# Sums by accumulating DMAs replaced by additions on GpSimd, in a gated scan with a feed-forward layer

## The chip, the cores and the metric

The kernel runs on one core of a Trainium2 chip. Five engines run their own instruction queues in order: TensorE (PE, with its weight loads PEld), VectorE (DVE), ScalarE (ACT), GpSimd (POOL) and SyncE (SP). An instruction that waits holds up all that stand behind it on its engine. The metric is the device time of one execution in microseconds (us).

## The reference

The first half is a gated scan along 6080 time steps, for 2 sequences of 256 channels; the second half is a feed-forward layer of 2048 hidden units on the 12160 resulting rows.

```python
sig = 1 / (1 + exp(-f_logit))
f = lower_bound + (1 - lower_bound) * sig
for t in range(S):
    h = f[:, t] * h + (1 - f[:, t]) * x[:, t]
    y[:, t] = h
h = y.reshape(B * S, D) @ w_in
g = h * clip(h + 3, 0, 6) / 6
out = g @ w_out
```

## The kernel before

Rows are handled as runs of 512 time steps (480 at the end) of one sequence; two runs of the same steps of both sequences make a pair. The first four runs go through the layer one by one (`direct`). Each of the ten later pairs goes through a 2x2 block product in seven multiplications where a plain one needs eight (`seven`), for the first product, and, for three of the eight blocks of hidden units in all pairs but the first, for the second product too (`chain`, `seven_in_banks`). Such a scheme multiplies sums and differences of blocks: t1, t2, t3 and t4, each made of blocks of x (the scan's result, tiles `xt`) or of g (the gated hidden units, tiles `r`).

Each operand is split into two parts of lower precision (`split`, `split_flat`): ACT writes the high part (`xhi`, `ghi`, `bhi`), DVE the rest (`xlo`, `glo`, `blo`), and PE multiplies three combinations. A product leaves PE in a bank of its accumulation memory (`bank`); ACT and DVE add or copy banks for the scheme (lines 628 to 640) and apply the gate (`gate`, lines 503 and 505), which frees the bank for a later product.

The sums are made in place, in one of two ways:

- t1 and t2 of g are additions by DVE (`ON_DVE`, line 811).
- t3 and t4 of g and all four sums of x are accumulating DMAs, issued by POOL (`add_into`, line 262). There are 4 per pair for x, 128 columns by 512 (480) values, 40 in all; and 4 per chain for g, two of them twice as long (1024 or 960 values), 36 in all.

The order of instructions on every engine is written by a planner (`ordered`): every job has an engine, a planning cost and a due time, and the planner walks through time, each engine taking the ready job that is due first. PE's jobs come in the order of the program's loops, with times to match. For an accumulating DMA the planner allows an issue (`ISSUE_ADD`), its bytes on a shared bus, a landing time and `LATE`, and it keeps the descriptors in flight below a limit. At the start PE runs multiplications of zeros (line 924) while it has nothing to do; their number follows from the plan.

Of the kernel before, what the change touches and what calls it, by code (L numbers as in the profile page):

```python
# [16 lines left out]
ALU = mybir.AluOpType  # L17
P = 128
BANK = 512
# [73 lines left out]
def dve_cost(n, per=1.0):  # L93
    return (151 + per * n) / 0.96


def pe_cost(n, count):
    return count * (n + 32) / 2.4

# [5 lines left out]
    return count * (4 * n + 64) / 2.4  # L105


HOP = {"PE": 230, "ACT": 70, "DVE": 70, "SP": 0, "POOL": 0}
ISSUE = 480
ISSUE_ADD = 1000  # L110
LATE = 1000
ON_DVE = {("t1", 0), ("t1", 1), ("t2", 0), ("t2", 1)}
AHEAD = 8000
DIRECT = 4
# [2 lines left out]
SCRATCH = 512  # L117
LANDING = 1700
SLOW_START = 6500
BYTES_PER_NS = 390  # L120
# [3 lines left out]
def ordered(jobs):  # L124


    for j in jobs:
        for b in j.bufs:
            if b.before is not None:
                j.needs.extend(u for u in b.before.users if u is not j)  # L130
    for j in jobs:
        j.needs = list(dict.fromkeys(j.needs))
        j.after = []
    for j in jobs:
        for n in j.needs:
            n.after.append(j)
    left = {j: len(j.after) for j in jobs}
    stack = [j for j in jobs if not left[j]]
    while stack:
        j = stack.pop()  # L140
        late = min((d.due for d in j.after), default=1e9) - HOP[j.engine] - j.cost
        if j.moves:
            late -= LANDING + j.moves / BYTES_PER_NS + (LATE if j.engine == "POOL" else 0)
        if j.at is None:
            j.due = late
        for n in j.needs:
            left[n] -= 1
            if not left[n]:
                stack.append(n)

    def early(j):
        return max(0.0, j.due - j.ahead) if j.due < 5e8 else 0.0
    missing = {j: len(j.needs) for j in jobs}
    ready = {e: [] for e in HOP}
    free = dict.fromkeys(ready, BEGIN)
    bus = 0.0
    flying = []
    number = {j: i for i, j in enumerate(jobs)}
    for j in jobs:
        if not missing[j]:  # L160
            ready[j.engine].append((early(j), j))
    order = []
    while any(ready.values()):
        best = None
        for e, waiting in ready.items():
            if waiting:
                start = max(free[e], min(r for r, _ in waiting))
                if best is None or start < best[0]:
                    best = (start, e)
        start, e = best  # L170
        could = [x for x in ready[e] if x[0] <= start]
        pick = min(could, key=lambda x: (x[1].due, number[x[1]]))
        ready[e].remove(pick)
        j = pick[1]
        if e == "POOL":
            room = SCRATCH // 16 - 1
            pieces = 1 + P // 16 * -(-j.moves // (2 * P * 2048))
            while flying and sum(k for _, k in flying) + pieces > room:
                start = max(start, flying.pop(0)[0])
        j.start = start  # L180
        free[e] = end = start + j.cost
        if j.moves:
            bus = max(bus, end)
            slow = min(j.moves / 250, max(0, SLOW_START - bus))
            bus += slow + (j.moves - 250 * slow) / BYTES_PER_NS
            end = bus + LANDING
            if e == "POOL":
                end += LATE
                flying.append((end, pieces))
        j.end = end  # L190
        order.append(j)
        for d in j.after:
            missing[d] -= 1
            if not missing[d]:
                at = max(n.end + (HOP[n.engine] if n.engine != d.engine else 0) for n in d.needs)
                ready[d.engine].append((max(at, early(d)), d))
    assert len(order) == len(jobs)
    return order
# [18 lines left out]
def gated_scan_then_ffn(  # L217
# [8 lines left out]
    nc = tc.nc  # L226
# [24 lines left out]
    def job(*args, **kw):  # L251
        j = Job(*args, **kw)
        jobs.append(j)
        return j
# [2 lines left out]
        engine = nc.scalar if queue == "ACT" else nc.sync  # L257
        return job(queue, ISSUE, lambda: engine.dma_start(out(), src), bufs=[buf] if buf else [], moves=size, ahead=EARLY)

    def add_into(size, out, src, needs, bufs, ahead=None):  # L260

        return job("POOL", ISSUE_ADD, lambda: nc.gpsimd.dma_start(out=out(), in_=src(), accum_op=ALU.add),  # L262
                   needs, bufs, moves=2 * size, ahead=ahead)

    r_ft = Ring(work, "ft", FT, [P, KD, BANK], F32)
    r_xt = Ring(work, "xt", 2, [P, KD, BANK], F32)
# [152 lines left out]
    def split(src, hi, lo, cut, n, needs, flip=False, to=None):  # L419

        to = to or cut

        def high():
            if flip:
                nc.scalar.mul(to(hi), cut(src), -1.0)  # L425
            else:
                nc.scalar.copy(to(hi), cut(src))  # L427

        def low():
            if flip:  # L430
                nc.vector.scalar_tensor_tensor(out=to(lo), in0=cut(src), scalar=-1.0, in1=to(hi).bitcast(F32),  # L431
                                               op0=ALU.mult, op1=ALU.subtract)
            else:
                nc.vector.tensor_tensor(to(lo), cut(src), to(hi).bitcast(F32), op=ALU.subtract)  # L434
        c = job("ACT", act_cost(n), high, needs, [src, hi])
        return [c, job("DVE", dve_cost(n), low, [c], [src, hi, lo])]
# [16 lines left out]
    def prep_pair(h, h2):  # L453


        n = runs[h][2]
        assert runs[h][0] == 0 and runs[h2][0] == 1
        _, xt, one = scan_x(h, [(0, n)])
        _, xt2, two = scan_x(h2, [(0, n)])
        ss, ss2 = one[0][-1], two[0][-1]  # L460

        def cut(k):
            return lambda b: b.get()[:, k, :n]

        def sum_into(buf, k, buf2, k2, needs):
            return [add_into(4 * n * P, lambda: cut(k)(buf), lambda: cut(k2)(buf2), needs, {buf, buf2})]
        both = lambda b: b.get()[:, :, :n]
        whole = lambda b: b.get()[:, :n]
        own, t12, t34 = [(r_xhi.new(), r_xlo.new()) for _ in range(3)]
        end = r_bhi.new(), r_blo.new()  # L470
        d_own = split(xt, *own, both, KD * n, ss)
        j1 = sum_into(xt, 0, xt2, 0, [*ss, *ss2, *d_own])
        d1 = split(xt, *t12, cut(0), n, j1)
        j3 = sum_into(xt2, 0, xt2, 1, [*ss2, *j1])
        j2 = sum_into(xt, 0, xt2, 1, [*d1, *ss2])
        d2 = split(xt, *t12, cut(0), n, j2, to=cut(1))
        d3 = split(xt2, *t34, both, KD * n, j3)
        j4 = sum_into(xt, 1, xt, 0, [*j2, *d_own])
        d4 = split(xt, *end, cut(1), n, j4, flip=True, to=whole)
        for name, bufs, at, done in (("b11", own, cut(0), d_own), ("b21", own, cut(1), d_own), ("b22", t34, cut(1), d3),  # L480
                                     ("t1", t12, cut(0), d1), ("t2", t12, cut(1), d2),
                                     ("t3", t34, cut(0), d3), ("t4", end, whole, d4)):
            operands[h, name] = bufs, at
            o_done[h, name] = done
# [5 lines left out]
    def pe(n, count, emit, needs, bufs, cost=pe_cost):  # L490
        j = job("PE", cost(n, count), emit, needs, bufs, at=clock[0])
        clock[0] += cost(n, count)
        return j
# [308 lines left out]
    def chain(h, h2):  # L802

        n = runs[h][2]
        r_ghi.left = r_glo.left = None
        made = g_done[h]
        flat = lambda b: b.get()[:, :(b.shape[1] // BANK) * n]

        def sum_into(name, z, out, x, needs, ahead=None):
            if (name, z) in ON_DVE:  # L810
                return job("DVE", dve_cost(n * (out.shape[1] // BANK)), lambda: nc.vector.tensor_tensor(flat(out), flat(out), flat(x), op=ALU.add),
                           needs, [out, x])
            return add_into(4 * (out.shape[1] // BANK) * n * P, lambda: flat(out), lambda: flat(x), needs, [out, x], ahead)
        ops = {}

        def operand(name, w, z, needs, flip):
# [5 lines left out]
        every = range(len(PARTS))  # L822
        d11 = [operand("b11", w11, z, g11, True) for z in every]
        t1 = [[sum_into("t1", z, w11[z], w12[z], [*g12[z], *d11[z]])] for z in every]
        dt1 = [operand("t1", w11, z, t1, False) for z in every]
        t3 = [[sum_into("t3", z, w12[z], w22[z], [*g22[z], *t1[z]], AHEAD)] for z in every]
# [78 lines left out]
    for _ in range(5):  # L905
        order = ordered(jobs)
        end = max(j.end for j in order)
        if best is None or end < best[0]:
            best = end, order, [(j.start, j.end) for j in order]
        for j in jobs:  # L910
            if j.at is not None:
                j.at = j.due = j.start
# [44 lines left out]
```

## Time and profile before

| | us |
|---|---|
| median of 3 runs (988.11 to 988.68) | 988.17 |
| the profiled execution | 988.75 |
| its span, from the first to the last instruction | 987.0 |
| PE busy | 980.0 |
| DVE busy | 842.2 |
| ACT busy | 705.3 |
| POOL busy | 66.9 |

The span is what the profile's views divide up; the profiled execution's own time has 1.75 us beside it. An engine's busy time is not a bound by itself: what matters is which engine the others end up waiting for. PE's clock is granted at full speed throughout the page's forty slices.

### The profile page before, as it was taken

The page shows a single profiled execution, that of the slowest core. Times are in us where ns is not written, and L with a number is a line of the kernel's source. Part 1 is how long each engine was busy: PE and PEld are TensorE (multiplying, and loading weights), DVE is VectorE, ACT ScalarE, POOL GpSimd, SP SyncE. Part 2 cuts the span into 40 slices and gives each one's busy share as a digit, 9 for nine tenths or more (in the row PEclk, how much of TensorE's full clock was granted, in tenths as well). Part 3 has the DMA queues.
Part 4 walks back from the last instruction along what each step waited for, and adds up shares of the span by engine and source line. Part 5 has one row for each costly group of instructions (what it writes and reads, how often), then busy time and mean ns, then how long its engine had stood idle before and what let it go on. Part 6 is the DMA issues. An engine that isn't in the chain of part 4 may idle for free.

```text
span 987.0 us, 11965 instructions
## 1 busy us (share of the span) xinstructions
PE 980.0 (99%) x4316; PEld 806.4 (82%) x4316; DVE 842.2 (85%) x1150; ACT 705.3 (71%) x1150; POOL 66.9 (7%) x80
## 2 busy tenths in 40 slices
PE   8999999999999999999999999999999999999998
PEld 3788888888888888888888888888888888888887
DVE  7999998679778979988988998898898898898883
ACT  7975666577667767768668767777776866876762
POOL 0000001000000100011011011010010101101100
PEclk9999999999999999999999999999999999999999
DMA  8842032021141233124116125224222412502301
GB/s 340 287 146 80 23 105 65 2 86 35 30 138 34 59 100 76 43 68 125 33 32 161 33 43 139 40 57 122 50 54 54 125 31 45 148 23 48 81 11 41
DMA packets 36843, 79.21 MB, mean 80 GB/s; under 512 B 3504, under 2 KB 9648, under 8 KB 36784
## 3 DMA queue, kind: packets, MB, share of 16 engines
q1 hardware_dynamic: 25424, 53.87, 16.1%
q0 software_dynamic: 10944, 24.32, 13.2%
q8 instruction: 34, 0.56, 0.2%
q10 hardware_dynamic: 416, 0.26, 0.1%
q14 instruction: 25, 0.20, 0.1%
HBM read 41.67 MB, written 12.45 MB: 55 GB/s over the span
## 4 chain that ended last, share of the span: by engine, by line
PE 98%; DVE 1%; ACT 0%; issue 0%
PE bank L649 51%; PE bank L538 38%; PE bank L604 8%; PE bank L614 1%; PE bank L535 0%; DVE xt L396 0%; DVE xt L406 0%; ACT r L384 0%; ACT r L393 0%; DVE r L505 0%; DVE r L577 0%; ACT last L413 0%
## 5 line engine op out<-in xcount | busy, mean ns | idle before, releaser
L503 ACT ACTIVATE r<-bank 128x512 f32<-128x512 f32 (+1 forms) x304 | 178.7, 591 | 118.6 <-PE bank L649 85.2
L505 DVE SCALAR_TENSOR_TENSOR r<-r,bank 128x512 f32<-128x512 f32 (+1 forms) x304 | 203.9, 676 | 48.1 <-ACT r L503 46.4
L649 PE MATMUL bank<-xhi,wst 128*128 128x512 f32 (+1 forms) x640 | 233.0, 387 | 0.0
L538 PE MATMUL bank<-ghi,whi 128*128 128x512 f32 (+1 forms) x548 | 212.7, 388 | 0.0
L538 PE MATMUL bank<-glo,whi 128*128 128x512 f32 (+1 forms) x548 | 212.5, 388 | 0.0
L538 PE MATMUL bank<-ghi,wlo 128*128 128x512 f32 (+1 forms) x548 | 212.4, 388 | 0.0
L431 DVE SCALAR_TENSOR_TENSOR glo<-r,ghi 128x1024 fp32r<-128x1024 f32 (+3 forms) x125 | 131.3, 1052 | 16.3 <-ACT ghi L425 16.1
L649 PEld LDWEIGHTS bank<-xhi,wst 128*128 128x128 f32 x640 | 120.1, 188 | 23.8
L427 ACT CAST ghi<-r 128x1024 fp32r<-128x1024 f32 (+3 forms) x107 | 98.7, 931 | 45.7 <-PE bank L649 31.1
L649 PE MATMUL bank<-xlo,wst 128*128 128x512 f32 (+1 forms) x320 | 123.8, 387 | 0.0
L425 ACT ACTIVATE ghi<-r 128x1024 fp32r<-128x1024 f32 (+3 forms) x125 | 115.3, 924 | 10.6 <-PE bank L538 5.3
L434 DVE TENSOR_TENSOR glo<-r,ghi 128x1024 fp32r<-128x1024 f32 (+3 forms) x107 | 113.8, 1073 | 10.5 <-ACT ghi L427 10.3
L538 PEld LDWEIGHTS bank<-ghi,wlo 128*128 128x128 f32 x548 | 102.8, 188 | 20.8 <-DVE wlo L311 0.2
L538 PEld LDWEIGHTS bank<-glo,whi 128*128 128x128 f32 x548 | 102.8, 188 | 20.7
L538 PEld LDWEIGHTS bank<-ghi,whi 128*128 128x128 f32 x548 | 102.9, 188 | 20.6 <-issue 0.2
L640 DVE TENSOR_TENSOR bank<-bank,e 128x512 f32<-128x512 f32 (+1 forms) x80 | 55.2, 690 | 21.0 <-PE bank L649 14.7
L262 POOL DMA_DIRECT2D xt<-xt x40 | 35.2, 880 | 556.4 <-ACT last L413 357.2
L649 PEld LDWEIGHTS bank<-xlo,wst 128*128 128x128 f32 x320 | 60.1, 188 | 12.0
L649 PE MATMUL bank<-ghi,wlo 128*128 128x512 f32 (+1 forms) x180 | 69.6, 387 | 0.0
L649 PE MATMUL bank<-ghi,whi 128*128 128x512 f32 (+1 forms) x180 | 69.6, 387 | 0.0
L649 PE MATMUL bank<-glo,whi 128*128 128x512 f32 (+1 forms) x180 | 69.6, 387 | 0.0
L638 DVE SCALAR_TENSOR_TENSOR e<-bank,e 128x512 f32<-128x512 f32 (+1 forms) x80 | 54.3, 679 | 10.4 <-PE bank L649 9.6
(105 smaller groups left out, 1494.2 us busy)
## 6 DMA issues: line engine op xcount, KB each, us to landing
outT<-r SPq DMA_DIRECT2D x40, 256.0 KB, 2.2
xt<-xT SPq DMA_DIRECT2D x18, 512.0 KB, 5.3
ft<-fT SPq DMA_DIRECT2D x17, 512.0 KB, 3.8
xt<-xt POOLq DMA_DIRECT2D x32, 256.0 KB, 3.2
wst<-w SPq DMA_DIRECT2D x14, 512.0 KB, 4.0
r<-r POOLq DMA_DIRECT2D x14, 512.0 KB, 4.8
wst<-w SPq DMA_DIRECT2D x14, 511.5 KB, 4.9
r<-r POOLq DMA_DIRECT2D x14, 256.0 KB, 3.4
```

The lines of the kernel that those rows point to most:

```text
L262: return job("POOL", ISSUE_ADD, lambda: nc.gpsimd.dma_start(out=out(), in_=src(), accum_op=ALU.add), needs, bufs, moves=2 * size, ahead=ahead)
L425: nc.scalar.mul(to(hi), cut(src), -1.0)
L427: nc.scalar.copy(to(hi), cut(src))
L431: nc.vector.scalar_tensor_tensor(out=to(lo), in0=cut(src), scalar=-1.0, in1=to(hi).bitcast(F32), op0=ALU.mult, op1=ALU.subtract)
L434: nc.vector.tensor_tensor(to(lo), cut(src), to(hi).bitcast(F32), op=ALU.subtract)
L503: b = job("ACT", act_cost(n, psum=True), lambda: nc.scalar.activation(piece(r, i, n), src.get()[:, :n], AF.Relu, bias=3.0, scale=-1.0 if n ...
L505: return job("DVE", dve_cost(n), lambda: nc.vector.scalar_tensor_tensor(out=piece(r, i, n), in0=piece(r, i, n), scalar=6.0, in1=src.get()[ ...
L538: nc.tensor.matmul(bank.get()[:, :n], wt[f][:, D + m * P:D + (m + 1) * P], piece(g, half, n), start=(start and i == 0), stop=(stop and i = ...
L604: nc.tensor.matmul(ph.get()[:, o:e], wt[f][:, k * P:(k + 1) * P], x[h].get()[:, k, o:e], start=(i == 0), stop=(i == len(ops) - 1),)
L638: nc.vector.scalar_tensor_tensor(out=o, in0=x, scalar=-1.0, in1=y, op0=ALU.mult, op1=ALU.subtract)
L640: nc.vector.tensor_tensor(o, x, y, op=ALU.add)
L649: nc.tensor.matmul(bank.get()[:, :n], wt(), x(), start=(start and z == 0 and i == 0), stop=(z == len(parts) - 1 and i == 2), skip_group_ch ...
```

## The change

The 76 accumulating DMAs become additions (`tensor_tensor`) that POOL carries out itself, with two operands from the on-chip buffer and the result in place of the first. In the planner their bytes, landing time, `LATE` and the limit on descriptors go; a POOL job now has a cost of its own (`pool_cost`) and a handover time.

```diff
+def pool_cost(n):
+    return 300 + 2.6 * n / 1.2
...
-HOP = {"PE": 230, "ACT": 70, "DVE": 70, "SP": 0, "POOL": 0}
+HOP = {"PE": 230, "ACT": 70, "DVE": 70, "SP": 0, "POOL": 70}
...
-ISSUE_ADD = 1000
-LATE = 1000
...
-    def add_into(size, out, src, needs, bufs, ahead=None):
-
-        return job("POOL", ISSUE_ADD, lambda: nc.gpsimd.dma_start(out=out(), in_=src(), accum_op=ALU.add),
-                   needs, bufs, moves=2 * size, ahead=ahead)
+    def add_into(n, out, src, needs, bufs, ahead=None):
+
+        return job("POOL", pool_cost(n), lambda: nc.gpsimd.tensor_tensor(out(), out(), src(), op=ALU.add),
+                   needs, bufs, ahead=ahead)
...
-            return [add_into(4 * n * P, lambda: cut(k)(buf), lambda: cut(k2)(buf2), needs, {buf, buf2})]
+            return [add_into(n, lambda: cut(k)(buf), lambda: cut(k2)(buf2), needs, {buf, buf2})]
...
-            return add_into(4 * (out.shape[1] // BANK) * n * P, lambda: flat(out), lambda: flat(x), needs, [out, x], ahead)
+            return add_into((out.shape[1] // BANK) * n, lambda: flat(out), lambda: flat(x), needs, [out, x], ahead)
```

The planner's numbers decide the order on every engine, so rows move on the others too. Three places follow; the number behind a name is that of the buffer.

POOL, the four sums of one chain (tiles `r`) and the first two sums of the next pair (tiles `xt`), before:

```order
L262 DMA r_3651<-r_3682 128x1024
L262 DMA r_3746<-r_3767 128x512
L262 DMA r_3799<-r_3736 128x512
L262 DMA r_3689<-r_3583 128x1024
L262 DMA xt_3787<-xt_3860 128x512
L262 DMA xt_3860<-xt_3860 128x512
```

and after:

```order
L255 TENSOR_TENSOR r_3617<-r_3617,r_3641 128x1024
L255 TENSOR_TENSOR r_3748<-r_3748,r_3765 128x512
L255 TENSOR_TENSOR r_3653<-r_3653,r_3599 128x1024
L255 TENSOR_TENSOR r_3793<-r_3793,r_3726 128x512
L255 TENSOR_TENSOR xt_3807<-xt_3807,xt_3882 128x512
L255 TENSOR_TENSOR xt_3882<-xt_3882 128x512
```

The sums keep their places but for the last two of the chain, which change order.

ACT at the same chain, where it splits t3 (`ghi_3939` of `r_3651`) and t4 (`ghi_3957` of `r_3689`, `ghi_3967` of `r_3799`), before:

```order
L393 ACTIVATE ft_3763<-ft_3763,gb,ga 128x512
L425 ACTIVATE ghi_3939<-r_3651 128x1024
L503 ACTIVATE r_3952<-bank_0_3873 128x512
L503 ACTIVATE r_3926<-e_3895 128x512
L427 CAST ghi_3957<-r_3689 128x1024
L427 CAST ghi_3967<-r_3799 128x512
L628 ACTIVATE bank_0_3975<-bank_0_3959 128x512
```

and after, with t3 in `ghi_3933` and t4 in `ghi_3952` and `ghi_3961`:

```order
L418 ACTIVATE ghi_3933<-r_3617 128x1024
L496 ACTIVATE r_3939<-bank_0_3872 128x512
L420 CAST ghi_3952<-r_3653 128x1024
L386 ACTIVATE ft_3791<-ft_3791,gb,ga 128x512
L420 CAST ghi_3961<-r_3793 128x512
L621 ACTIVATE bank_0_3969<-bank_0_3957 128x512
```

One gate (L503 of `r_3926`) and the scan's line 393 have moved from ahead of the split of t4 to other places; the split stands nearer to its sum.

ACT at the start of the program, where it prepares the weights (`xhi_110`, `xhi_117`; lines 300, 302) and the gate of the second run (`r_121`; lines 384, 393), before:

```order
L310 CAST whi_69<-xhi_110 128x256 [waits DVE_49]
L300 ACTIVATE xhi_117<-xhi_117 128x256 [waits DMAHW7_49,DMAHW0_49]
L302 ACTIVATE xhi_117<-xhi_117 128x256 [waits Activation_49]
L413 ACTIVATE last<-xt_108 128x1 [waits DVE_49]
L384 ACTIVATE r_121<-r_121 128x1024 [waits DMAHW1_49]
L393 ACTIVATE r_121<-r_121,gb,ga 128x512 [waits Activation_49]
```

and after:

```order
L303 CAST whi_69<-xhi_110 128x256 [waits DVE_49]
L377 ACTIVATE r_117<-r_117 128x1024 [waits DMAHW7_49]
L386 ACTIVATE r_117<-r_117,gb,ga 128x512 [waits Activation_49]
L293 ACTIVATE xhi_119<-xhi_119 128x256 [waits DMAHW1_49,DMAHW0_49]
L295 ACTIVATE xhi_119<-xhi_119 128x256 [waits Activation_49]
```

The second run's gate goes ahead of the second block of weights; SP issues their loads in the same new order, and two of the 41 multiplications of zeros on PE are gone.

## Rows read from the trace of the kernel before

**Rows 1.** The page: busy time, share of the span, instructions.

```profile
PE 980.0 (99%) x4316; PEld 806.4 (82%) x4316; DVE 842.2 (85%) x1150; ACT 705.3 (71%) x1150; POOL 66.9 (7%) x80
```

**Rows 2.** Waits of PE: for whom, us in total, times, longest.

```profile
PE bank L614 <- DVE xhi L307: 1.6, 1, 1.6
PE bank L924 <- DVE spare_w L918: 1.2, 1, 1.2
PE bank L614 <- DVE r L505: 0.5, 1, 0.5
```

**Rows 3.** Busy time by stretch, one pair: PE, PEld, DVE, ACT, POOL, clock.

```profile
449.00:528.00 79.00, 79.00 (x350) 65.46 (x349) 69.72 (x89) 58.38 (x94) 7.00 (x8) 1.00 0.30 72
```

**Rows 4.** POOL's groups: busy us, mean ns, idle before them and its releaser.

```profile
L262 POOL DMA_DIRECT2D xt<-xt x40 | 35.2, 880 | 556.4 <-ACT last L413 357.2 <-ACT r L503 101.3 <-DVE xlo L434 42.1
L262 POOL DMA_DIRECT2D r<-r x36 | 31.5, 875 | 313.5 <-DVE r L505 198.8 <-DVE glo L434 88.3 <-DVE glo L431 26.4
```

**Rows 5.** DMA issues by POOL: count, KB each, median us to landing.

```profile
xt<-xt POOLq DMA_DIRECT2D x32, 256.0 KB, 3.2
r<-r POOLq DMA_DIRECT2D x14, 512.0 KB, 4.8
```

**Rows 6.** ACT's longest waits for DMAs.

```profile
ACT ghi L427 <- DMA r<-r: 0.4, 1, 0.4
```

**Rows 7.** DVE's groups by form: busy us, mean ns.

```profile
L505 DVE SCALAR_TENSOR_TENSOR r<-r,bank 128x512 f32<-128x512 f32 x256 | 173.1, 682 | 38.7 <-ACT r L503 37.3
L505 DVE SCALAR_TENSOR_TENSOR r<-r,e 128x512 f32<-128x512 f32 x64 | 43.6, 683 | 3.9 <-ACT r L503 3.1
L811 DVE TENSOR_TENSOR r<-r,r 128x1024 f32<-128x1024 f32 x14 | 17.1, 1222 | 0.3
L811 DVE TENSOR_TENSOR r<-r,r 128x512 f32<-128x512 f32 x14 | 9.7, 691 | 0.4
```

**Rows 8.** Timeline of POOL from 419 to 461: start, us, instruction.

```profile
419.65 0.89 POOL L262 DMA_DIRECT2D xt<-xt  x1 [3.98 <-DVE xlo L434]
...
440.77 0.88 POOL L262 DMA_DIRECT2D r<-r  x1 [16.63 <-DVE r L505]
...
460.69 0.87 POOL L262 DMA_DIRECT2D r<-r  x1 [2.79 <-DVE glo L431]
```

**Rows 9.** Timeline of DVE around the three.

```profile
419.16 0.68 DVE L505 SCALAR_TENSOR_TENSOR r<-r,e 128x512 f32<-128x512 f32 x1
419.76 1.22 DVE L434 TENSOR_TENSOR glo<-r,ghi 128x1024 fp32r<-128x1024 f32 x1
420.90 0.68 DVE L505 SCALAR_TENSOR_TENSOR r<-r,bank 128x512 f32<-128x512 f32 x1
...
441.24 1.32 DVE L505 SCALAR_TENSOR_TENSOR r<-r,bank 128x512 f32<-128x512 f32 x2
...
460.28 0.70 DVE L640 TENSOR_TENSOR bank<-bank,e 128x512 f32<-128x512 f32 x1 [0.51 <-PE bank L649]
460.89 0.68 DVE L431 SCALAR_TENSOR_TENSOR glo<-r,ghi 128x512 fp32r<-128x512 f32 x1
...
464.36 0.69 DVE L638 SCALAR_TENSOR_TENSOR e<-bank,e 128x512 f32<-128x512 f32 x1 [0.40 <-PE bank L649]
...
466.10 0.68 DVE L505 SCALAR_TENSOR_TENSOR r<-r,bank 128x512 f32<-128x512 f32 x1
```

**Rows 10.** Timeline of PE: the products that take those banks next.

```profile
423.36 0.39 PE L649 MATMUL bank<-xhi,whi 128*128 128x512 f32 x1
...
467.56 0.39 PE L649 MATMUL bank<-xhi,wst 128*128 128x512 f32 x1
```

**Rows 11.** Timeline of ACT at the start.

```profile
10.33 0.45 ACT L300 ACTIVATE xhi<-xhi 128x256 f32<-128x256 f32 x1
...
11.91 1.04 ACT L384 ACTIVATE r<-r 128x1024 f32<-128x1024 f32 x1
```

**Rows 12.** Timeline of PE: the second run's first product.

```profile
18.06 1.99 PE L614 MATMUL bank<-xt,xhi 128*128 128x512 f32 x4 [0.46 <-DVE r L505]
```

More of the change, by code (lines that the diff above doesn't have):

```diff
@@ L142, in ordered @@
         if j.moves:
-            late -= LANDING + j.moves / BYTES_PER_NS + (LATE if j.engine == "POOL" else 0)
+            late -= LANDING + j.moves / BYTES_PER_NS
         if j.at is None:
@@ L156, in ordered @@
     bus = 0.0
-    flying = []
     number = {j: i for i, j in enumerate(jobs)}
@@ L174, in ordered @@
         j = pick[1]
[L175 to L179, printed above, removed]
         j.start = start
@@ L186, in ordered @@
             end = bus + LANDING
-            if e == "POOL":
-                end += LATE
-                flying.append((end, pieces))
         j.end = end
```

## Prediction

> **What bounds the kernel now.** I read the page first: PE is busy for 980.0 of 987.0 us, DVE for 842, ACT for 705, POOL for 67 [rows 1]. Busy PE alone proves little, so the waits of PE came next: it waits three times in all, 3.3 us together, and always on line 614 or 924, which stand in the first 20 us [rows 2]. From then on PE is never without an operand or a bank. The view by stretches says the same of one pair in the middle: in 79.0 us PE is busy for 79.0 at a granted clock of 1.00, and DVE for 69.7, so DVE has 9.3 us to spare per pair [rows 3]. Two things follow. What is taken off POOL and the DMA queues can return almost nothing, since PE waits for neither. And whatever makes DVE or ACT later than PE can bear is paid in full, since PE has no slack to make it up.
>
> **What the change removes.** 76 issues on POOL go, 40 for x and 36 for g, some 0.88 us each, 66.7 us together [rows 4], and the transfers that landed 3.2 us (short) or 4.8 us (long) after issue [rows 5]. POOL sat idle for most of the span and nobody waited for its issues; of the landings ACT waited for one, for 0.4 us [rows 6], and PE for none. I count the removal at nothing: the cover is PE's own work, and were it gone it would show up among PE's waits.
>
> **What it adds on POOL.** 76 additions: 40 for x and 18 for g of 512 (480) values, 18 for g of 1024 (960). No row shows POOL adding. The nearest row from below is DVE's addition of the same shape, 0.69 and 1.22 us [rows 7]; from above, the DMA's landing, 3.2 and 4.8 us, since the plan lived with it. These lie far apart and I take the middle on a scale of ratios, 1.5 us (the root of 0.69 times 3.2) and 2.4 us (the root of 1.22 times 4.8). POOL would be busy for 58 x 1.5 + 18 x 2.4 = 130 us, 13% of the span, so it is far from a bound, and a sum would be ready earlier than a DMA's. In the order ACT's splits stand closer behind their sums than before, so some of that lead is spent, but I see no term in it: the sum costs half of what it did.
>
> The Trainium skill, GPSIMD Engine Reference, section 3 (Performance versus the Vector engine), gives 4497 ns for a two-input addition of 2048 values and a slope of about 2.6 cycles per value; scaled down that is an estimate of 1.2 and 2.3 us, and by it the sum below would be 6.2 us in place of 7.1. No run here shows it yet.
>
> **What it adds on DVE.** This is the term. POOL reads two operands from the on-chip buffer for 1.5 to 2.4 us at a time, right beside DVE instructions that do the same. Whether both can run at once the trace does not show, as POOL computes nothing in it. The lower end is nothing: they run side by side, as ACT and DVE do now. The upper end is that a DVE instruction with both operands in the buffer stands until the addition is over; one with an operand in a bank (r<-r,bank; 682 ns, against 683 ns for r<-r,e today [rows 7]) would go on. I take the upper end, as the one that PE would notice, and keep the lower as a rival.
>
> The Trainium skill, SBUF — State Buffer, section "Who interferes with whom", states this upper end: VectorE's second operand comes through a read interface shared with GpSimd, and the one that comes second waits for the whole instruction of the other. No row here can confirm it.
>
> Laid over the trace, a long sum that starts at 460.69 [rows 8] would end at 463.09. DVE's line 640 at 460.28 has an operand in a bank and goes on; the next, glo<-r,ghi at 460.89, has not, and stands for 463.09 - 460.89 = 2.20 us, with everything behind it. DVE's idle 0.40 us before 464.36 takes that to 1.80. Line 505 at 466.10 ends at 466.78 and frees a bank that PE's product at 467.56 takes [rows 9, 10]: a lead of 0.78. So PE stands for 1.80 - 0.78 = 1.02 us there.
>
> A short sum at 419.65 [rows 8] would start when r<-r,e has finished, at 419.84, and end at 421.34; glo<-r,ghi at 419.76 would stand for some 1.5 us. Line 505 at 420.90 would end 1.5 us after 421.58, and PE takes its bank at 423.36: a lead of 1.78, and PE waits for nothing [rows 9, 10]. I count short sums at nothing; the cover is this lead, and without it each costs up to 1.5 us.
>
> There are nine chains, with two long sums each; one of the two meets splits and short leads as at 460.69, the other, here at 440.77, falls on gates with an operand in a bank, 441.24 and on, and holds up nothing [rows 8, 9]. Seven chains are of 512 columns; the last two, of 480, have shorter sums, and I take them at nothing. The sum is 7 x 1.02 = 7.1 us.
>
> **What moves at the start.** ACT takes the second run's gate (11.91) ahead of the second block of weights (10.33), up to 1.6 us earlier [rows 11], and PE's wait of 0.46 us before 18.06 hangs on that run [rows 12]. Against it the second block of weights comes later, 1.04 us and more, and its products with it. Between a gain of 1.6 + 0.46 = 2.1 us and a loss of about 1.0 I take nothing.
>
> So the profiled execution's 988.75 (987.0 of span and 1.75 beside it) would become 995.9; it lay 0.6 above the median of 988.17, and from the median the forecast is 988.17 + 7.1 = 995.3.
>
> **The rivals.**
>
> *Side by side, or covered.* POOL's additions do not hold DVE up, or its leads of up to 1.8 us cover all of it. For it: the one short place above is covered, and DVE has 9.3 us to spare per pair against 6 x 1.5 + 2 x 2.4 = 13.8 us of POOL's work, only part of which meets DVE instructions of the wrong kind. Against it: the place at 460.69, which comes in every chain. Time: 988.2.
>
> *DVE runs full.* If nearly all of the 13.8 us per pair is DVE's to stand, it exceeds the 9.3 us to spare by 4.5, and nine pairs cost 9 x 4.5 = 40 us: about 1028. The point from which it decides is a stall of 9.3 us per pair, an average of 1.2 us for each of the eight sums. Against it: DVE spends a good part of its time on instructions with an operand in a bank, 173.1 us on r<-r,bank of 512 values alone [rows 7], and my short place and long place give 1.5 and 2.2 only because they meet the other kind at once.
>
> *Faster.* The start alone: the second run's gate comes 1.6 us earlier, PE's 0.46 us go, and every later product moves up by 2.1 us, while the sums cost nothing: 986.1. It decides only if the new load order keeps the weights in time. For it: two multiplications of zeros fewer. Against it: PE's longest wait at the start, 1.6 us, is for weights (line 307) [rows 2], which this order delays.
>
> **How the numbers follow.** Forecast 0.57, side by side or covered 0.27, DVE full 0.10, faster 0.06. The low end is the rival of the start less some of its gain, 986.8. The high end lets one short sum in each of ten pairs find no lead: 988.17 + 7.1 + 10 x 1.5 = 1010. About 1.5 in 10 is left out, most of it above. What this kernel's measurement can tell from no change is about 0.2%, 2 us. The second case and a small part of the first stay within that, 0.30; the rival of the start goes beyond it by very little, 0.05 faster; the rest is slower, 0.65.
>
> **What would show each step.** Right: 76 POOL additions of 1 to 3 us; among DVE's groups those with two operands in the buffer (glo<-r,ghi at lines 424 and 427, r<-r,e) have a higher mean or a tail of single long ones beside POOL's rows, while r<-r,bank keeps 0.68 us; PE has waits for DVE at line 642 in the chains, about 1 us each, after 195 us. Wrong by the first rival: the DVE means stand and PE's waits remain those of the first 20 us. Wrong by the second: DVE busy near 79 us per pair, and PE waits at most sums. What else would make it wrong: additions of over 3 us on POOL, so that ACT's splits wait for POOL with the gates queued behind them, or a first addition that comes late for a reason no row here shows.

## The result, and the profile after

The changed kernel takes 994.64 us (median of four runs, 994.55 to 994.69); the kernel before, run beside it, takes 988.25 (988.11 to 988.68). The ratio is 1.0064 with a 95% interval of 1.0046 to 1.0081: 6.4 us slower, well beyond the 0.2% that can be told here. The profiled run of the changed kernel took 994.67, of which 992.8 are its span. The code has become seven lines shorter above all that matters here, so line 642 below is line 649 of before, 498 is 505, 424 and 427 are 431 and 434, 631 and 633 are 638 and 640, and the additions stand on line 255.

The page's first line answers to [rows 1]:

```profile
PE 985.8 (99%) x4314; PEld 804.5 (81%) x4314; DVE 883.0 (89%) x1150; ACT 707.1 (71%) x1150; POOL 144.9 (15%) x80
```

DVE has gained 40.8 us with not one instruction more, POOL 78. PE is "busy" for 5.8 us more with two records fewer. That is a trap: a product's record lasts 0.39 us while the next starts 0.23 us behind it, so a start that comes up to 0.16 us late leaves no gap between the records and counts as busy, and so does part of any longer delay. The waits of PE hardly show the loss; those of its weight loads, which wait for the same banks, do. First PE, which answers to [rows 2], then PEld; each row is for whom it waited, us in total, times, longest:

```profile
PE bank L917 <- DVE spare_w L911: 1.2, 1, 1.2
PE bank L642 <- DVE r L498: 0.7, 1, 0.7
```

```profile
PEld bank L642 <- DVE r L498: 3.9, 10, 1.2
PEld bank L642 <- DVE e L631: 2.7, 7, 0.4
```

The kernel before has no wait of PE or PEld on this line for DVE behind the start. Now there are two kinds above all: ten for line 498 and seven for line 631, both of which read a bank that a product wants next.

The chain of work that ended last gives the sizes. Its largest pieces start once in each pair of runs, at the same product. In the kernel before it is:

```profile
289.53 27.20 PE bank L649 x120
...
448.68 27.20 PE bank L649 x120
...
766.92 27.20 PE bank L649 x120
```

and in the changed kernel:

```profile
289.21 26.65 PE bank L642 x117
...
449.96 18.36 PE bank L642 x81
468.34 8.50 PE bank L642 x36
...
772.40 26.95 PE bank L642 x117
```

From the first to the last of these, six pairs take 477.39 us before and 483.19 after, 5.80 more: 0.97 us a pair on the mean, and nearly all of the loss. Where the piece of 120 is broken in two, at 468.34, something has stepped in between.

Where the loss arises can be read product by product. The order on PE has moved with the plan too: at 1209 of the 4275 places behind the multiplications of zeros, another product stands than before. But run 2 below, which takes the time of before (988.30), has the changed kernel's order at all 4275, so each product's start in the changed kernel can be set against its start there. The changed kernel falls behind in two kinds of place:

| where | falls behind there (us) | together (us) |
|---|---|---|
| the sums of x, in six pairs | 0.54, 0.53, 0.26, 0.26, 1.42, 0.53 | 3.5 |
| the long sums of g, in six chains | 0.33, 0.29, 0.31, 0.29, 0.30, 0.38 | 1.9 |

The places in the second row are gone in run 9, where the long sums are halved. The other 0.8 of 6.3 us are steps of 0.1 us or less.

### The profile page after: what moved, and what is told of

The parts are those of the page before. It is cut to its first block, busy times and chain, and to the rows that moved or that the text cites. A ratio compares the mean times of both kernels' runs of the same rounds, so it can differ in the third digit from the quotient of the medians.

```text
span 992.8 us, 11796 instructions
## 1 busy us (share of the span) xinstructions
PE 985.8 (99%) x4314; PEld 804.5 (81%) x4314; DVE 883.0 (89%) x1150; ACT 707.1 (71%) x1150; POOL 144.9 (15%) x80
## 4 chain that ended last, share of the span: by engine, by line
PE 89%; DVE 6%; ACT 2%; issue 1%; DMA 0%; POOL 0%; DVEq 0%; ACTq 0%; POOLq 0%; SPq 0%
PE bank L642 47%; PE bank L531 33%; PE bank L597 8%; DVE xt L399 1%; DVE glo L424 1%; DVE xlo L427 1%; DVE xt L389 1%; PE bank L607 1%; DVE r L498 1%; DVE glo L427 1%; ACT ft L386 1%; ACT ft L377 0%; DMA ft<-fT 0%; PE bank L528 0%; DVE e L631 0%
## 5 line engine op out<-in xcount | busy, mean ns | idle before, releaser
L642 PE MATMUL bank<-xhi,wst 128*128 128x512 f32 (+1 forms) x640 | 235.4, 389 | 0.8 <-DVE r L498 0.7
L424 DVE SCALAR_TENSOR_TENSOR glo<-r,ghi 128x1024 fp32r<-128x1024 f32 (+3 forms) x125 | 156.5, 1256 | 21.1 <-ACT ghi L418 20.9
L427 DVE TENSOR_TENSOR glo<-r,ghi 128x1024 fp32r<-128x1024 f32 (+3 forms) x107 | 123.4, 1168 | 9.4 <-ACT ghi L420 8.8
L255 POOL TENSOR_TENSOR r<-r,r 128x1024 f32<-128x1024 f32 (+3 forms) x36 | 75.6, 2111 | 312.4 <-DVE r L498 217.0
L531 PEld LDWEIGHTS bank<-glo,whi 128*128 128x128 f32 x548 | 102.8, 188 | 21.2 <-DVE glo L424 0.7
L255 POOL TENSOR_TENSOR xt<-xt,xt 128x512 f32<-128x512 f32 (+1 forms) x20 | 30.0, 1501 | 479.9 <-DVE xt L399 347.2
L642 PEld LDWEIGHTS bank<-xlo,wst 128*128 128x128 f32 x320 | 60.1, 188 | 11.5
```

The lines of the kernel that those rows point to most:

```text
L255: return job("POOL", pool_cost(n), lambda: nc.gpsimd.tensor_tensor(out(), out(), src(), op=ALU.add), needs, bufs, ahead=ahead)
L531: nc.tensor.matmul(bank.get()[:, :n], wt[f][:, D + m * P:D + (m + 1) * P], piece(g, half, n), start=(start and i == 0), stop=(stop and i = ...
L642: nc.tensor.matmul(bank.get()[:, :n], wt(), x(), start=(start and z == 0 and i == 0), stop=(z == len(parts) - 1 and i == 2), skip_group_ch ...
```

## Where DVE and POOL stand for each other

The four short sums of x in one pair, on POOL and then the same stretch on DVE, from the timelines (start, duration, instruction, idle time before it):

```profile
413.24 1.28 POOL L255 TENSOR_TENSOR xt<-xt,xt 128x512 f32<-128x512 f32 x1 [29.46 <-DVE xlo L427]
414.61 2.16 POOL L255 TENSOR_TENSOR xt<-xt 128x512 f32<-128x512 f32 x1
417.40 1.30 POOL L255 TENSOR_TENSOR xt<-xt,xt 128x512 f32<-128x512 f32 x1 [0.63 <-DVE xlo L427]
418.78 2.15 POOL L255 TENSOR_TENSOR xt<-xt 128x512 f32<-128x512 f32 x1
```

```profile
413.59 2.02 DVE L427 TENSOR_TENSOR glo<-r,ghi 128x1024 fp32r<-128x1024 f32 x1
415.53 0.68 DVE L498 SCALAR_TENSOR_TENSOR r<-r,bank 128x512 f32<-128x512 f32 x1
416.13 1.19 DVE L427 TENSOR_TENSOR xlo<-xt,xhi 128x512 fp32r<-128x512 f32 x1
417.24 0.68 DVE L498 SCALAR_TENSOR_TENSOR r<-r,bank 128x512 f32<-128x512 f32 x1
417.84 1.94 DVE L424 SCALAR_TENSOR_TENSOR glo<-r,ghi 128x1024 fp32r<-128x1024 f32 x1
419.70 0.68 DVE L631 SCALAR_TENSOR_TENSOR e<-bank,e 128x512 f32<-128x512 f32 x1
```

The split at 413.59 starts inside the first addition and lasts 2.02 us, where its like takes 1.22: the addition ends at 414.52, and 1.09 us later the split does. This holds beyond the one place: of the 22 splits of 1024 values that start during an addition, 21 end 1.08 to 1.09 us after its end, whether they lasted 1.44 or 2.97 us; the other started within 0.03 us of the addition and went first. Now the other way round: POOL's second addition starts at 414.61 and lasts 2.16 us where its like takes 1.28, and it ends 1.16 us after the split. So the one that comes second stands until the other's instruction is over. An instruction with an operand in a bank, 0.68 us beside the same additions, does not stand at all.

The chain of work of that stretch goes through DVE, where in the kernel before it is PE alone:

```profile
413.68 1.93 DVE glo L427
...
419.78 0.61 DVE e L631
420.39 0.04 issue
420.44 0.96 PE bank L642 x3
```

The three stalls, 0.80, 0.51 and 0.72 us, add up to 2.0, and with no idle time between them they all reach line 631, whose bank PE wants. On PE this reads:

```profile
419.92 0.41 PE L531 MATMUL bank<-glo,whi 128*128 128x512 f32 x1
420.44 0.50 PE L642 MATMUL bank<-bhi,whi 128*128 128x512 f32 x1
420.77 0.40 PE L642 MATMUL bank<-blo,whi 128*128 128x512 f32 x1
```

Starts 0.52 and 0.33 us apart instead of 0.23: 0.4 us gone, and no wait is written beside the rows.

One of the six places of x is dearer, and it goes another way. POOL's first sum of that pair, held up by a split that started 0.03 us behind it, takes 2.39 us; ACT waits 3.71 us for it, DVE 1.24 us for ACT, and PE's product starts 1.12 us behind the one before it:

```profile
654.95 2.39 POOL L255 TENSOR_TENSOR xt<-xt,xt 128x512 f32<-128x512 f32 x1 [30.15 <-DVE xlo L427]
657.38 0.62 ACT L420 CAST xhi<-xt 128x512 fp32r<-128x512 f32 x1 [3.71 <-POOL xt L255]
658.03 1.23 DVE L427 TENSOR_TENSOR xlo<-xt,xhi 128x512 fp32r<-128x512 f32 x1 [1.24 <-ACT xhi L420]
659.91 0.50 PE L642 MATMUL bank<-xhi,wst 128*128 128x512 f32 x1 [0.74 <-DVE r L498]
```

Here a sum does come late, for some 0.9 us of the 6.4.

The long sum of a chain that the prediction laid out from [rows 8, 9]: POOL's long addition and a short one behind it, then DVE, then PE at the product of line 642 that [rows 10] showed at 467.56:

```profile
459.19 2.78 POOL L255 TENSOR_TENSOR r<-r,r 128x1024 f32<-128x1024 f32 x1 [10.62 <-DVE glo L427]
461.93 2.27 POOL L255 TENSOR_TENSOR r<-r,r 128x512 f32<-128x512 f32 x1
```

```profile
460.41 2.64 DVE L424 SCALAR_TENSOR_TENSOR glo<-r,ghi 128x1024 fp32r<-128x1024 f32 x1
...
463.58 1.18 DVE L424 SCALAR_TENSOR_TENSOR glo<-r,ghi 128x512 fp32r<-128x512 f32 x1
...
467.61 0.68 DVE L498 SCALAR_TENSOR_TENSOR r<-r,bank 128x512 f32<-128x512 f32 x1
```

```profile
467.93 0.39 PE L642 MATMUL bank<-xhi,wlo 128*128 128x512 f32 x1
468.34 0.50 PE L642 MATMUL bank<-xhi,wst 128*128 128x512 f32 x1
468.68 0.40 PE L642 MATMUL bank<-xlo,wst 128*128 128x512 f32 x1
```

The first split stands behind the long addition, for 2.64 - 1.22 = 1.42 us, the second behind the short one, for 1.18 - 0.68 = 0.50, together 1.92, where 2.20 was laid out for the long one alone. Line 498 ends at 468.29, and PE's product follows at 468.34, 0.41 us after the one before in place of 0.23, and the next 0.34 after that: 0.29 us lost here, not 1.02.

Grouped by form, the rows of DVE and POOL say the same of the whole run (busy us, mean ns):

```profile
L498 DVE SCALAR_TENSOR_TENSOR r<-r,bank 128x512 f32<-128x512 f32 x256 | 172.7, 679 | 22.4 <-ACT r L496 21.0
L424 DVE SCALAR_TENSOR_TENSOR glo<-r,ghi 128x1024 fp32r<-128x1024 f32 x71 | 102.8, 1449 | 7.1 <-ACT ghi L418 6.9
L427 DVE TENSOR_TENSOR xlo<-xt,xhi 128x512 fp32r<-128x512 f32 x18 | 18.3, 1015 | 1.2 <-ACT xhi L420 1.2
L255 POOL TENSOR_TENSOR r<-r,r 128x1024 f32<-128x1024 f32 x14 | 35.2, 2513 | 215.3 <-DVE r L498 140.4 <-DVE glo L427 74.9
```

With a bank: 679 ns, 682 before [rows 7]. With both operands in the buffer: 1449 and 1015, where the kernel before has 1217 for the first form and 685 for the second.

## The experiments

Three theories stood against each other. **A**: DVE stands behind POOL's additions, as just read. **B**: the sums come late, ACT's splits wait for POOL, and what is queued behind them is late too; the changed kernel does show ACT's xhi waiting 15.2 us in 12 waits for POOL, where the kernel before has no wait for a sum of x. **C**: the order that the planner made with the new costs is worse by itself.

All ratios are to the kernel before on the same chip, with their 95% intervals. The line numbers in each edit's trace are those of the kernel it was made from, or a line or so on. The edits are cut to the instruction or number that changes; a job's other arguments are left out.

**1. The old order, with POOL's additions.** In the kernel before, only the instruction is exchanged; planner and costs stay.

```
-  lambda: nc.gpsimd.dma_start(out=out(), in_=src(), accum_op=ALU.add),
+  lambda: nc.gpsimd.tensor_tensor(out(), out(), src(), op=ALU.add),
```

> The order of before on every engine, made for accumulating DMAs, with POOL additions in the DMAs' places; the result is unchanged. Theories: (A) DVE stands behind POOL's additions where both read two operands from the buffer; (B) the sums come late for the new plan, ACT waits for them and gates queue behind it; (C) the new order itself costs. A: still a loss, DVE busy 870 to 895 us as in the changed kernel, time 991 to 998. B: the old order leaves every sum some 5 us, so nobody waits for POOL: 988. C: 988.

Measured: 994.60, ratio 1.0062 [1.0049, 1.0074], DVE busy 881.8, and ACT waits for POOL nowhere. A loss of the same size is there without the new order and without one wait of ACT for a sum, so neither B nor C is needed for it.

**2. The new order, with additions of 8 values.**

```
-  nc.gpsimd.tensor_tensor(out(), out(), src(), op=ALU.add)
+  nc.gpsimd.tensor_tensor(out()[:, :8], out()[:, :8], src()[:, :8], op=ALU.add)
```

> The changed kernel's order, with each addition cut to its first 8 columns (the sums are left incomplete). A: POOL is hardly busy, DVE goes back to 842 us busy and the time to about 988. B: the sums are early, so also about 988. C: the order stays, so 994 to 995.

Measured: 988.30, ratio 1.0000 [0.9991, 1.0008], DVE 843.3, POOL 21.2. The sums are left incomplete, but the order is the changed kernel's. It costs nothing, and gains nothing either: C falls as a cause.

**3. POOL as busy, but reading nothing.** Each addition becomes three memsets of its output.

```
-  nc.gpsimd.tensor_tensor(out(), out(), src(), op=ALU.add)
+  [nc.gpsimd.memset(out(), 0.0) for _ in range(3)]
```

> The changed kernel's order, each addition replaced by three fills of the sum's tile with zeros (the sums are left out): POOL is busy for a time of the same kind but reads nothing. A: DVE's groups go back to 1.22 and 0.69 us, DVE busy 840 to 850, time 987.5 to 989. B: if POOL's three fills take as long as an addition, ACT waits as before and the time stays at 992 to 995. C: 994 to 995.

Measured: 988.43, ratio 0.9999 [0.9990, 1.0008]. POOL is busy for 140.1 us, almost as with the additions, and ACT waits for it 11.5 us, but DVE has 843.8 and its splits are back at 1220 ns:

```profile
L424 DVE SCALAR_TENSOR_TENSOR glo<-r,ghi 128x1024 fp32r<-128x1024 f32 x71 | 86.5, 1220 | 11.4 <-ACT ghi L418 11.2
```

So it is not POOL's time alone, and lateness of this size costs nothing: what is gone is that POOL reads. A memset is also shorter than an addition, 0.53 us beside 1.28 for 512 values; run 10 takes that apart.

**4. A plan that counts on later sums.** The planner's fixed cost of a POOL addition goes from 300 to 2000 ns, so that it sets what uses a sum further behind it.

```
-    return 300 + 2.6 * n / 1.2
+    return 2000 + 2.6 * n / 1.2
```

> The changed kernel with 1.7 us more planned for each addition, so that the splits stand later behind their sums; the result is unchanged. A: ACT's waits for POOL shrink but DVE still stands, busy 870 to 895 us; time 991 to 997. B: ACT's waits for POOL (15 us in the changed kernel) vanish and the time falls to 988 to 989.5. C: another order again, not foretold.

Measured: 991.62, ratio 1.0032 [1.0019, 1.0044]. DVE's total is nearly as large as in the changed kernel, 881.2, and ACT no longer waits for POOL; B had expected 988 to 989.5 for that. The waits of PEld for line 631 are gone; those for the chains' line 498 remain, 4.0 us in 7. Such a place on DVE and on PE:

```profile
459.28 2.85 DVE L424 SCALAR_TENSOR_TENSOR glo<-r,ghi 128x1024 fp32r<-128x1024 f32 x1 [0.72 <-ACT ghi L418]
...
467.88 0.68 DVE L498 SCALAR_TENSOR_TENSOR r<-r,bank 128x512 f32<-128x512 f32 x1
```

```profile
468.01 0.39 PE L642 MATMUL bank<-bhi,wlo 128*128 128x512 f32 x1
468.61 0.50 PE L642 MATMUL bank<-xhi,wst 128*128 128x512 f32 x1 [0.22 <-DVE r L498]
468.95 0.40 PE L642 MATMUL bank<-xlo,wst 128*128 128x512 f32 x1
```

The products follow each other 0.60 and 0.34 us apart: the price is 0.37 + 0.11 = 0.48 us. The first split's stall is 2.85 - 1.22 = 1.63. Set against run 8, which has the same products in the same order, six chains lose 0.49 us each, nearly all of the 3.3. This run separates the two places: with the x sums' place gone, half the loss is gone, and DVE's busy time has not moved. What DVE stands in sum does not decide; how much of it meets at a bank that PE wants next does.

**5 and 6. One kind of sum at a time.** In the kernel before, the sums of x alone (5) or of g alone (6) become additions on POOL, the rest stay DMAs; the planner's cost and hop for POOL go with the kind. The core of both edits:

```
+        if pool:
+            return job("POOL", 300 + 2.6 * size / (4 * P) / 1.2, lambda: nc.gpsimd.tensor_tensor(
+                out(), out(), src(), op=ALU.add), needs, bufs, ahead=ahead)
```

> The four sums of x per pair are POOL's additions, those of g stay accumulating DMAs, each planned as in the two kernels; the result is unchanged. A (DVE stands behind POOL's additions): only short additions, 40 of some 1.3 us, DVE busy 855 to 865 us; where PE's leads of 1 to 2 us cover them the time stays within 1 us of 988.3, and if the x places of the changed kernel (0.4 us in most pairs) come back it is 990 to 992.

> The four sums of g per chain are POOL's additions, those of x stay accumulating DMAs; the result is unchanged. A: the long additions hold up glo<-r,ghi by up to 1.5 us just ahead of the gate that frees the bank of the next product; 0.3 to 0.5 us in each of seven chains, 990 to 992. The prediction's own 1.02 per chain would be 995.

Measured: x alone 991.57, ratio 1.0034 [1.0022, 1.0047], with PEld's waits for line 631's counterpart as in the changed kernel (2.7 us in 7). g alone 993.60, ratio 1.0054 [1.0042, 1.0067], with PEld waiting 5.0 us in 7 for the counterpart of line 498 and none for that of 631. Both kinds cost, at a place of their own. 3.3 and 5.3 do not add up to 6.4. Run 6 has the products in the order of before; set against them, four of its chains lose 0.68 us each, two others 0.44 and 0.73, one 0.22, and a product of the last pair, at 941.64, 0.87. In the changed kernel a chain loses 0.29 to 0.38, while the six places of x cost 2.8 us in run 5 and 3.5 there. So it is the long sums that are dearer alone; that this comes of the other order, or of a PE that is already late at one place and has more lead at the next, is argued and not shown.

**7. The same sums on DVE.**

```
-  return job("POOL", ISSUE_ADD, lambda: nc.gpsimd.dma_start(out=out(), in_=src(), accum_op=ALU.add),
+  return job("DVE", dve_cost(size / (4 * P)), lambda: nc.vector.tensor_tensor(out(), out(), src(), op=ALU.add),
```

> All 76 sums are additions by DVE, as t1 and t2 are; the result is unchanged. DVE gains 58 x 0.69 + 18 x 1.22 = 62 us of its own and no longer shares with POOL: busy some 900 us, more than in the changed kernel (883). If what counts is how full DVE is, the time is above the changed kernel's 994.6; if what counts is that the plan does not know of the standing, the plan places this work and the time is 988 to 991.

Measured: 999.02, ratio 1.0109 [1.0095, 1.0122], DVE 891.8. Where DVE makes the sums itself, it loses 49.6 us; POOL's additions cost it 40.8 without its making any. Standing for POOL, DVE gives up four fifths of the time that the sums would take it, though 4.4 us are still saved at the end. Here the plan knows of all of DVE's work, and the time is yet above the changed kernel's, as the first reading had it: that the plan knows of the work is not enough here.

**8. The later plan, and long sums in two halves.** The plan of run 4, and each addition of 1024 or 960 values as two of half the size, so that a waiting DVE instruction gets its turn between them.

```
+  [nc.gpsimd.tensor_tensor(out()[:, o:o + w], out()[:, o:o + w], src()[:, o:o + w], op=ALU.add)
+   for o in range(0, n, w)]      # w stands here for n, or n / 2 where n is over 512
```

> The late plan (1.7 us more planned for each addition) with each long addition of g issued as two of half the length, in the same order on every engine; the result is unchanged. A: no stall is longer than a short addition, some 1.3 us in place of 2.4, which the lead at the chain's place covers, so most of the late plan's 3.3 us goes: 988.3 to 989.5, unless POOL takes its second half before DVE has had a turn, which would leave 991.6. If the loss lay in the order, 991.6 as well.

Measured: 988.22, ratio 0.9999 [0.9990, 1.0008]. The split that took 2.85 us beside a whole addition takes 1.74 beside a half, and PE's piece of the chain is not broken any more, in every pair of 512 columns:

```profile
458.47 1.74 DVE L424 SCALAR_TENSOR_TENSOR glo<-r,ghi 128x1024 fp32r<-128x1024 f32 x1 [0.72 <-ACT ghi L418]
```

```profile
448.55 26.52 PE bank L642 x117
```

POOL is busier than ever, 152.7, DVE has 875.1, and the time is that of before. It does not beat it.

**9. The halves alone**, in the changed kernel's own plan.

> The changed kernel with its own plan, each long addition of g issued as two of half the length; the result is unchanged. A (DVE stands behind POOL's additions, and PE pays where the stall outlasts its lead): the chain places of the changed kernel, some 2 us together, go, those at the sums of x (0.4 us a pair, 0.9 once) stay: 991.5 to 993. If the whole gain of the halves on the late plan came from the later splits: 994.6.

Measured: 991.88, ratio 1.0036 [1.0022, 1.0049]. The chains' places are mended, the x sums' place is not (PEld waits for line 631 again, 2.7 us in 7). Runs 4 and 9 each take one half of the loss away, run 8 both.

**10. POOL reading one operand.** Two copies instead of one addition.

```
-  nc.gpsimd.tensor_tensor(out(), out(), src(), op=ALU.add)
+  [nc.gpsimd.tensor_copy(out(), src()) for _ in range(2)]
```

> The changed kernel's order, each addition replaced by two copies of the second operand into the sum's tile (the additions are left out): POOL reads one operand and not two. If any read by POOL holds up a DVE instruction with two operands in the buffer, DVE is busy 860 to 890 us and the time 990 to 996; if only two-operand reads do, DVE goes back to 843 and the time to 988.3, as with the fills.

Measured: 988.63, ratio 1.0003 [0.9995, 1.0012]; DVE 853.2, line 424's split 1273 ns. POOL is busy for 155.8 us, more than with the additions, and DVE stands for a quarter as long: between what the two readings of A expected. The rows tell why. Two copies in the stretch of x's sums, and the split beside them, from the timelines of POOL and DVE:

```profile
416.59 0.62 POOL L255 COPY xt<-xt 128x512 f32<-128x512 f32 x1
416.68 1.59 DVE L424 SCALAR_TENSOR_TENSOR glo<-r,ghi 128x1024 fp32r<-128x1024 f32 x1
417.27 1.49 POOL L255 COPY xt<-xt 128x512 f32<-128x512 f32 x1
```

The split stands until the copy is over, at 417.21, and ends 1.07 us later, as behind an addition; then the next copy stands for the split. Of 22 splits of 1024 values that start during a copy, 20 end 1.07 to 1.08 us after it (the other two started within 0.03 us of it and went first). So a read of one operand holds DVE up as fully as one of two. The stalls are short because a copy is short, 0.62 us for 512 values where an addition takes 1.28, and because DVE gets its turn between the two. ACT waits for POOL for 24.0 us, more than in the changed kernel, and no loss is to be seen: the waits of ACT as such are not the cause, and B is left with the one place at 659.91.

**11. Each addition twice.**

```
-  nc.gpsimd.tensor_tensor(out(), out(), src(), op=ALU.add)
+  [nc.gpsimd.tensor_tensor(out(), out(), src(), op=ALU.add) for _ in range(2)]
```

> The changed kernel's order, each addition made twice in a row (the sums get their second operand twice): POOL is busy for 240 to 290 us. A: DVE stands about twice as long, busy 905 to 930 us, and the excess over PE's leads more than doubles: 1002 to 1015. If DVE's turns between two additions keep every single stall as it was, ACT's waits for POOL grow and the time is 996 to 1003.

Measured: 1061.47, ratio 1.0740 [1.0725, 1.0755], outside what either theory expected. DVE's surplus over the kernel before is near to twice that of the changed kernel (87.8 us, 40.8), but the loss is eleven times as large. PE now waits for ACT as well as for DVE:

```profile
PE bank L642 <- DVE r L498: 18.1, 20, 2.2
PE bank L642 <- ACT bank L621: 16.7, 9, 2.0
PE bank L642 <- DVE bank L633: 7.7, 10, 1.2
```

ACT waits for POOL here for 63.1 us at xhi and 13.2 at ghi, so with sums twice as long B's lateness may have come on top; PE's granted clock is 0.98 from 449 to 528, where the changed kernel has 1.00. What each of these costs was not taken apart.

## Why the prediction was right, step by step

**What bounds the kernel**: right. PE had no slack, and every delay that reached a bank it wanted was paid.

**The removal at nothing**: right. In run 2 the DMAs are gone and the additions are as good as gone, and the time is 988.30. ([rows 6] shows ACT's one wait for a sum's landing; its waits for loads of `ft`, 9.5 us in all, were longer.)

**POOL's prices**: near. Taken were 1.5 and 2.4 us and 130 in all; the mean of a short sum lies between 1.48 and 1.97 us by form, of a long one at 2.51, in all 144.9. The shortest of 512 values is 1.283 us. At the places shown, what is above it is POOL's own standing, which the prediction let happen once, for 0.19 us at 419.65, and put into no price.

**DVE stands if both operands are in the buffer**: right, by runs 1 to 3 and by the rows. The Trainium skill's page SBUF — State Buffer, section "Who interferes with whom", states just this rule, for a GpSimd instruction that reads the buffer. The trace agrees: a split beside an addition takes 2.02 us for 1.22, one beside a copy 1.59, one beside memsets, which read nothing, 1.22. The estimates worked out from the Trainium skill's GPSIMD Engine Reference, section 3, 1.2 us for a short sum and 2.3 for a long one, lie a little under the shortest rows, 1.283 and 2.395 us; with 2.3 the prediction's sum would have come to 6.4, not to the 6.2 given there.

**7 x 1.02 for the long sums**: the stall comes near (1.92 us in place of 2.20, though of a long and a short addition together), the price to PE does not. Measured are 0.29 us at 468.34 and 1.9 in all, where 7.1 were put. In run 6, which keeps PE's order of before, four chains of seven lose 0.68, still two thirds of 1.02. The plan also starts the addition elsewhere, at 459.19 and not at 460.69; how much of the difference comes of that, and how much of products that arrive late themselves, was not taken apart.

**Short sums at nothing**: this is the step that failed. I laid out one sum beside one split and set its stall against one lead of 1.78 us. The four x sums of a pair come one behind the other, every split among them stands, and 0.80 + 0.51 + 0.72 = 2.0 us pile up before line 631. They cost 3.5 us in the changed kernel, and run 5, x alone, costs 3.3. The two errors cancel, and that is luck: the mechanism was right, but the larger part of the loss comes from the term put at nothing, and the only term of the sum brought about a quarter of what it was to bring.

**The start at nothing**: right within half a microsecond. The product at 289.53 of before is at 289.21 here, so 0.3 us were gained up to there.

**The sum**: 995.3 forecast, 994.64 measured; 7.1 and 6.4 us. That they lie so close is owed to the two errors above.

**The rivals.** Side by side or covered: PE's waits on line 642 and DVE's 883.0 speak against it, but its cover is real where the plan gives it, as run 8 shows. DVE full: DVE rose by 3.6 us in the pair from 449, to 73.36 of 79, far from full; its point was 9.3. Faster by the start: the 0.3 us were there, far from 2.1, and the sums ate them.

What stays open is why the doubled additions cost so much more than twice (run 11), and why a chain loses 0.68 us with g's sums alone and 0.3 with both kinds at once; that the two kinds add up to 8.6 against 6.4 is measured, the reasons given at runs 5 and 6 are only argued.

## What to carry to other kernels

Work moved to an idle GpSimd is not free to VectorE: ask of each VectorE instruction whether it reads two operands from the buffer while GpSimd reads one or more, and lay the stalls of a whole stretch one behind the other against the lead of the next bank, not one by one. The busy share (89%) does not tell the price; two kernels with 881 us of DVE differ by 3 us, and one with 875 loses nothing. Where the additions must be on GpSimd, cut long ones in two and let the plan count on them later: together that gave back all 6.4 us, each alone about half; the accumulating DMAs had held up nobody but ACT, once, for 0.4 us.

## What the runs showed of the hardware

The standing is mutual: a short addition takes 1.28 us alone and 2.15 when a DVE split of 1.2 us has the operands. DVE's waiting instruction goes ahead between two of POOL's that follow each other at once, which is why halves help: in run 8 the split that starts at 458.47 takes 1.74 us in place of 2.85. Three memsets of 512 values (526 ns each) hold DVE up by nothing. A copy, which reads one operand, holds it up until it is over, as an addition does, but it is over sooner (0.62 us for 512 values), so that two copies in place of each addition cost DVE a quarter as much (843.3 us busy with next to no additions, 853.2 with copies, 883.0 with additions).
